# Queries and keys cast to bf16 in the DMA on GpSimd's queue and turned by single heads; values alone on SyncE's queue

## The chip, the cores and the metric

The kernel runs on one core of a Trainium2 chip. The metric is the device time of that core in microseconds (us), the median of several executions. Kernels are compared only within the same rounds. PE is TensorE, PEld its weight loads, DVE VectorE, ACT ScalarE, POOL GpSimd, SP SyncE.

## The reference, cut to what matters

Chunked attention with a few memory keys, then a Fourier mix of the whole batch entry, then an MLP:

```python
# q, k, v: (4, 8, 768, 64) fp32; mem_k, mem_v: (4, 8, 8, 64)
for c in range(24):                          # chunks of 32 queries
    k_full = concat(mem_k, k[l_start:r_end])   # 16 keys to the left, 8 to the right
    a = softmax(q_c @ k_full.T / 8)
    out[c] = a @ concat(mem_v, v[l_start:r_end])
x = out as (4, 768, 512)                     # heads side by side
u = x + real(fft2(x))                        # over sequence and model dimension
un = (u - mean) / sqrt(var + 1e-6)
out = u + relu(un @ w_ch1) @ w_ch2           # 512 -> 2048 -> 512
```

## The kernel before

Heads are worked in 16 pairs, four for each of the four batch entries ("batches"). Each task of an engine (a load, a cast, a turn, which is a transpose on TensorE, a product) is handed to a scheduler with a cost and its conditions; the scheduler fixes one static order for each engine. Within a batch the attention feeds the Fourier mix (DVE folds, TensorE products `ps`), and that the MLP (`ph` is the first product, `pc` the second). The MLP of batch 0 runs beside the attention of batch 1, and so on. Names in the traces: `trq` and `trk` are turned queries and keys, `va` values, `sc` scores, `e` exponentials, `xa` their products with the values, `xsb` the normalised sums; `zy`, `pq`, `ff`, `hi`, `lo` are steps of the folds. A PSUM bank, or bank, is one of the buffers that the kernel takes with `bank(...)` for TensorE's products (`trq`, `sc`, `xa`, `ps`, `ph` and others). The parts that matter here:

```python
def e_load_q(n):                     # e_load_k alike; both on SyncE's queue
    nc.sync.dma_start(qf[n % NS], q[...])              # fp32, 3 buffers
def e_load_v(n, hh):                 # also SyncE: 3 value pieces, the memory's values
    ...
def e_cast_q(n, eng):                # DVE in batch 0, GpSimd later; e_cast_k alike
    eng.tensor_copy(qb_of[n].rearrange(cp_b), qf[n % NS]...)   # fp32 -> bf16, one buffer
def e_overlap(n, hh):                # the rows that neighbouring chunks share
    nc.gpsimd.tensor_copy(v1[0:32, 1:NB, 0:D + 1], v1[96:128, 0:NT, 0:D + 1])
def e_turn_q(n):                     # 8 matmuls, both heads at once: 128 weight columns
    for j in range(RB):
        nc.tensor.transpose(trq[:, j*QP:(j+1)*QP], qb[:, j] as (p, h d), ident_b[...])
...
w2_sb = wpool.tile([P, NHT, DM], FP16)           # second MLP weight
va.append(w2_flat[...])                          # values of pair 3 lie in the same memory
W2_AT = (1, 1)                                   # w2 asked for with the second pair of batch 1
```

The softmax here doesn't subtract the row's maximum and nothing guards it: scores larger than these inputs give would overflow.

## Time and profile before

| | before |
|---|---|
| device time, median of 3 first runs | 317.24 us |
| span of the profiled run | 315.9 us |
| mean granted TensorE clock in it | 0.978 |
| PE / DVE / ACT / POOL busy | 295.4 / 188.1 / 168.8 / 80.7 us |
| first softmax exponential | 19.76 us |
| first MLP matmul | 56.41 us |
| waits of `pc` for `w2` | 3.6 us |

TensorE's busy share of 94% says little on its own. Early in the run it holds dummy matmuls that compute nothing (`warm`, 236 in the groups). I therefore read the time at milestones: the first exponential (the attention begins), the first MLP matmul (from there TensorE has real work nearly always), and each wait of TensorE behind it. A timeline line reads: start, length, engine, source line, operation, output<-input, shape, how many in a row, and in brackets the idle time before it with its releaser. The prediction below shows the lines of before.

### The profile page before, as it was taken

How to read it: one execution, taken by the hardware profiler on the slowest of the kernel's cores; microseconds unless marked ns; L12 is line 12 of the kernel's file. 1: busy time of each engine (PE TensorE's matmuls, PEld its weight loads, DVE VectorE, ACT ScalarE, POOL GpSimd, SP SyncE). 2: the span in 40 equal slices, each digit the busy share in tenths (PEclk: the TensorE clock that was granted, in tenths of full speed). 3: DMA queues.
4: the chain of work that ended last, by engine and by line, in shares of the span. 5: the costliest groups of instructions: out<-in, count | busy, mean ns of one | idle time of the engine just before them, and what ended most of it. 6: DMA issues, size and time to landing. Idle time of an engine off the chain costs nothing.

```text
span 315.9 us, 7464 instructions
## 1 busy us (share of the span) xinstructions
PE 295.4 (94%) x3129; PEld 197.9 (63%) x3129; DVE 188.1 (60%) x367; ACT 168.8 (53%) x302; POOL 80.7 (26%) x97
## 2 busy tenths in 40 slices
PE   8489899977999979999799999999999999999994
PEld 8488899644667656686466665666764554554541
DVE  8977989601454989789999598975940101002001
ACT  8778435873768844548547462851482270540710
POOL 6442811853333749333800001000020000000000
PEclk9779999999999979999899999999999999999999
DMA  7995999995397999253200000001000100101001
GB/s 191 193 174 116 245 211 211 191 246 102 81 196 145 193 187 208 63 161 95 58 0 2 35 0 36 35 0 66 2 33 29 74 0 37 65 0 68 33 33 66
DMA packets 41888, 30.68 MB, mean 97 GB/s; under 512 B 30080, under 2 KB 32128, under 8 KB 41856
## 3 DMA queue, kind: packets, MB, share of 16 engines
q1 hardware_dynamic: 35712, 19.73, 30.8%
q0 software_dynamic: 2688, 4.19, 7.5%
q10 hardware_dynamic: 3456, 6.29, 5.2%
q8 instruction: 24, 0.39, 0.6%
q14 instruction: 8, 0.07, 0.1%
HBM read 28.11 MB, written 6.29 MB: 109 GB/s over the span
## 4 chain that ended last, share of the span: by engine, by line
PE 73%; DVE 18%; DMA 5%; ACT 2%; issue 1%; DVEq 0%
PE pc L649 26%; PE ph L635 22%; PE ps L479 7%; PE xa L405 6%; PE pm L514 5%; DMA w_sb<-in_moe_w_ch_dram 5%; PE sc L380 2%; DVE xsb L416 2%; DVE zy L439 2%; DVE yS L689 1%; PE trk L359 1%; PE warm L428 1%; PE trq L346 1%; PE tp L614 1%; DVE pq L447 1%
## 5 line engine op out<-in xcount | busy, mean ns | idle before, releaser
L642 ACT ACTIVATE hT<-ph 128x384 f16<-128x384 f32 x128 | 62.0, 492 | 59.1 <-PE ph L635 58.4
L635 PE MATMUL ph<-unT,w_sb 128*128 128x384 f16 x512 | 90.7, 330 | 2.0 <-DVE unT L620 1.3
L649 PE MATMUL pc<-w_sb,hT 128*128 128x512 f16 x384 | 88.7, 379 | 3.6 <-DMA w_sb<-in_moe_w_ch_dram 3.6
L655 DVE SCALAR_TENSOR_TENSOR osb<-pc,rstd,xsb 128x512 f32<-128x512 f32 x24 | 18.0, 750 | 88.6 <-PE pc L649 88.5
L635 PEld LDWEIGHTS <-w_sb 128*128 128x128 f16 x512 | 49.1, 99 | 34.2 <-issue 4.5
L649 PEld LDWEIGHTS <-hT 128*128 128x128 f16 x384 | 36.0, 98 | 42.9 <-issue 4.1
L340 POOL COPY va<-va 32x780 f32<-32x780 f32 x30 | 32.6, 1097 | 39.1 <-DMA va<-in_v_dram 32.0
L392 ACT ACTIVATE e<-sc,mbias 128x384 f32<-128x384 f32 x62 | 32.7, 582 | 14.7 <-PE sc L380 14.5
L405 PEld LDWEIGHTS xa<-va,e 128*64 128x64 f32 x720 | 23.9, 140 | 8.0 <-issue 4.1
L405 PE MATMUL xa<-va,e 128*64 128x65 f32 x720 | 28.0, 229 | 0.0
L608 ACT ACTIVATE un<-xsb,mu_s 128x512 f16<-128x512 f32 x18 | 13.0, 721 | 16.4 <-DVE mu_s L602 16.3
L428 PE MATMUL warm<-zeros 128*128 128x128 bf16 x236 | 19.3, 247 | 1.0 <-DVE zero L246 1.0
L336 POOL CAST kb<-kf 104x1024 bf16<-104x1024 f32 x12 | 13.4, 1120 | 22.8 <-PE trk L359 10.8
L626 POOL TENSOR_SCALAR rstd<-mu_s 128x6 f32<-128x6 f32 x4 | 1.0, 245 | 71.4 <-DVE mu_s L602 71.3
L416 DVE TENSOR_TENSOR xsb<-xa,zs 128x384 f32<-128x384 f32 x32 | 17.8, 557 | 1.1
L428 PEld LDWEIGHTS <-zeros 128*128 128x128 bf16 x236 | 17.1, 113 | 1.4 <-DVE zero L246 1.0
L494 ACT CAST up<-ps 128x386 f16<-128x386 f32 x16 | 9.6, 601 | 14.9 <-PE ps L479 14.9
L332 POOL CAST qb<-qf 96x1024 bf16<-96x1024 f32 x12 | 13.3, 1106 | 15.2 <-PE xa L405 7.5
L601 DVE BATCH_NORM_STATS2 st<-xsb 128x6 f32<-128x512 f32 x24 | 16.5, 686 | 0.5
L467 ACT CAST hi<-ff 128x768 f16<-128x768 f32 x14 | 11.4, 833 | 9.7 <-DVE ff L560 6.7
L369 ACT COPY kTb<-trk 128x832 bf16<-128x832 bf16 x16 | 13.7, 856 | 5.1 <-PE trk L359 3.3
L351 ACT COPY qT<-trq 128x768 bf16<-128x768 bf16 x16 | 12.8, 802 | 6.1 <-PE sc L380 4.6
(134 smaller groups left out, 401.4 us busy)
## 6 DMA issues: line engine op xcount, KB each, us to landing
qf<-in_q_dram SPq DMA_DIRECT2D x16, 384.0 KB
kf<-in_k_dram SPq DMA_DIRECT2D x16, 384.0 KB
out_dram<-osb ACTq DMA_DIRECT2D x24, 256.0 KB
va<-in_v_dram SPq DMA_DIRECT2D x30, 176.0 KB
w_sb<-in_moe_w_ch_dram POOLq DMA_DIRECT2D x8, 512.0 KB, 12.1
va<-in_mem_v_dram SPq DMA_DIRECT2D x30, 24.0 KB
va<-in_v_dram SPq DMA_DIRECT2D x15, 28.0 KB
w_sb<-in_v_dram SPq DMA_DIRECT2D x2, 176.0 KB
```

Source lines behind the costliest of these rows:

```text
L340: nc.gpsimd.tensor_copy(v1[0:32, 1:NB, 0:D + 1], v1[96:128, 0:NT, 0:D + 1])
L392: nc.scalar.activation(e1[:, :, :, ts(half, 32)], sc[:, :, 0:6, ts(half, 32)], AFT.Exp, bias=mbias[:, half:half + 1], scale=1.0 / math.sqr ...
L405: nc.tensor.matmul(xa[64 * half:64 * half + 64, st, hh, 0:65], e1[:, hh, t6, :], v1[:, 6 * g + t6 + 1, 0:65], start=True, stop=True)
L416: nc.vector.tensor_tensor(xs[b][:, 3 * g:3 * g + 3, 2 * pr * D:(2 * pr + 2) * D] .rearrange("p s (h d) -> p s h d", h=2), xa[:, :, :, 0:D] ...
L428: nc.tensor.matmul(warm_of[0], zeros, zeros, start=True, stop=True)
L479: nc.tensor.matmul(out_[:, sp, :], part[:, ab, sp * 3 + st, c0:c1], tab[:, sp, st, :], start=(first and sp + st + i == 0), stop=(last and ...
L514: nc.tensor.matmul(pm[:, par, :], lhs, rhs[:, par, :], start=(im == 0), stop=(im == 3))
L601: nc.vector.bn_stats(st6, xs[b][:, kt, :])
L635: nc.tensor.matmul(ph[:, 0:384], w1_sb[:, dt, ts(ht, P)], unT_of[b][:, dt, sh * 384:(sh + 1) * 384], start=(dt == 0), stop=(dt == NDT - 1))
L642: nc.scalar.activation(hT_of[b, sh][:, ht, :], ph_of.pop((b, sh, ht))[:, 0:384], AFT.Relu, bias=0.0, scale=-1.0)
L649: nc.tensor.matmul(pc_of[b, sh, stl], hT_of[b, sh][:, ht, ts(stl, P)], w2_sb[:, ht, :], start=(ht == 0), stop=(ht == NHT - 1))
L655: nc.vector.scalar_tensor_tensor(osb, pc_of.pop((b, sh, stl)), rstd_of[b][:, st:st + 1], xs[b][:, st, :], ALU.mult, ALU.add)
```

## The change

Its intent: let the DMA cast queries and keys, so that neither DVE (batch 0) nor GpSimd (later) casts; keep four pairs in flight instead of three; leave SyncE's queue to the values; take the values' last tile out of the fixed memory of `w2`, and load `w2` earlier. The price is that the DMA leaves the two heads side by side in another order, so each head is turned by itself: 16 matmuls with 64 weight columns for each turn instead of 8 with 128.

```diff
-    NS = 3
+    NS = 4
-    qf = [spool.tile([QP, 2, RB * D], FP32, ...)]     # kf alike
+    qf = [spool.tile([QP, 2, RB * D], BF16, ...)]     # kf: slices of one tile
 def e_load_q(n):                                      # e_load_k alike
-        nc.sync.dma_start(qf[n % NS], ...)
+        nc.gpsimd.dma_start(qf[n % NS], ...)
-    def e_cast_q(n, eng): ...
-    def e_cast_k(n, eng): ...
 def e_turn_q(n):                                      # e_turn_k alike
-            nc.tensor.transpose(trq[:, j*QP:(j+1)*QP], qb[:, j] as (p, h d), ...)
+            for hh in range(2):
+                nc.tensor.transpose(trq[64*hh:64*hh+64, j*QP:(j+1)*QP],
+                                    qb[:, hh, ts(j, D)], ident_b[0:QP, 0:QP])
 ...
-    t_rows = ...                      # GpSimd's clears of value tiles came before the tables
+    # clears moved to ACT, SyncE (a DMA) and behind GpSimd's table rows
+        behind1 = kept["ov"] if n == HP else None
+    done = {0: fourier(0)}
+    t_w2 = load_w2(kept["f0"])
-            if (b, i) == W2_AT:
-                t_w2 = load_w2(kept["ov"])
```

More of the change, by code (lines that the diff above doesn't have):

```diff
@@ L173 @@
     bps = ctx.enter_context(tc.tile_pool(name="banks", bufs=1, space=bass.MemoryType.PSUM))
-    NS = 3
+    NS = 4
     HP = H // 2
-    qf = [spool.tile([QP, 2, RB * D], FP32, name=f"qf{i}") for i in range(NS)]
-    kf = [spool.tile([KP, 2, RB * D], FP32, name=f"kf{i}") for i in range(NS)]
+    qf = [spool.tile([QP, 2, RB * D], BF16, name=f"qf{i}") for i in range(NS)]
+    kf_all = spool.tile([KP, NS, 2, RB * D], BF16)
+    kf = [kf_all[:, i] for i in range(NS)]
     NV = 3
@@ L186 @@
            for pr in ((0, 3, 1, 2) if b == 0 else (0, 2, 1, 3))]
-    plan = Plan(dict(qf=NS, kf=NS, va=NV, kTb=NKT, qb=1, kb=1, qT=2, tr=2, sc=1, xa=2, e1=3,
+    plan = Plan(dict(qf=NS, kf=NS, va=NV, kTb=NKT, qT=2, tr=2, sc=1, xa=2, e1=3,
                      xsb=3, fold=2, hl=1, up=4, dn=4, acc=4, mlp=3, un=3, unT=2, hT=1, osb=3), 6)
@@ L196 @@
     MLPS = 1000000
+    QT_DVE = (1, 2)
     NPR = B * H // 2
@@ L212 @@
     sv0 = cpool.tile([P, 1], FP32)
+    gate = cpool.tile([1, 1], FP32)
     zero = cpool.tile([P, 1], FP32)
@@ L232 @@
     w1_sb = wpool.tile([P, NDT, DFF], FP16)
-    w2_sb = wpool.tile([P, NHT, DM], FP16)
-    w2_flat = w2_sb.rearrange("p a b -> p (a b)")
-    va.append(w2_flat[:, 0:4 * NB * 66].bitcast(FP32)
-              .rearrange("p (h b c) -> p h b c", h=2, c=66))
-    e1_last = (w2_flat[:, 4 * NB * 66:4 * NB * 66 + 4 * 6 * 64].bitcast(FP32)
-               .rearrange("p (h t c) -> p h t c", h=2, c=64))
+    last = wpool.tile([P, 2, NB * 66 + 6 * 64], FP32, tag="w2", name="last")
+    va.append(last[:, :, 0:NB * 66].rearrange("p h (b c) -> p h b c", c=66))
+    e1_last = last[:, :, NB * 66:].rearrange("p h (t c) -> p h t c", c=64)
+    w2_of = []
     def va_at(n):
@@ L272, in e_scales, with e_clear_kf @@
         nc.vector.tensor_scalar(svD, sv[:, 0:1], 1.0 / DM, None, ALU.mult)
+    def e_clear_kf():
+        for p0, p1 in ((0, 7), (7 + QP, KP)):
+            nc.sync.dma_start(kf_all[p0:p1].rearrange("p i h (j d) -> p (i h j) d", d=P),
+                              zeros[0:p1 - p0].unsqueeze(1).to_broadcast(
+                                  [p1 - p0, NS * 2 * RB * D // P, P]))
     def e_clear_act(t):
-        flat = t if len(t.shape) == 2 else t.rearrange("p a b -> p (a b)")
-        nc.scalar.copy(flat, zero[0:flat.shape[0]].to_broadcast(list(flat.shape)))
+        nc.scalar.copy(t, zero[0:t.shape[0]].unsqueeze(2).to_broadcast(list(t.shape)))
     def e_rows_of_ones():
@@ L300, in e_load_q @@
         b, pr = seq[n]
-        nc.sync.dma_start(qf[n % NS],
+        nc.gpsimd.dma_start(qf[n % NS],
                           q[b, 2 * pr:2 * pr + 2].rearrange("h (p j) d -> p h (j d)", j=RB))
@@ L305, in e_load_k @@
         b, pr = seq[n]
-        nc.sync.dma_start(kf[n % NS][7:7 + QP],
+        nc.gpsimd.dma_start(kf[n % NS][7:7 + QP],
                           k[b, 2 * pr:2 * pr + 2].rearrange("h (p j) d -> p h (j d)", j=RB))
@@ L323, in e_load_v @@
                           mem_v[b, 2 * pr + hh].unsqueeze(1).to_broadcast([NMEM, NT, D]))
-    qT_of, kT_of, qb_of, kb_of, tr_of, e1_of, sc_of, xa_of, xs = ({} for _ in range(9))
-    cp_q = "p h (j d) -> p h j d"
-    cp_b = "p j h d -> p h j d"
-    def e_cast_q(n, eng):
-        qb_of[n] = apool.tile([QP, RB, 2, D], BF16, tag="qb", bufs=1, name="qb")
-        eng.tensor_copy(qb_of[n].rearrange(cp_b), qf[n % NS].rearrange(cp_q, j=RB))
-    def e_cast_k(n, eng):
-        kb_of[n] = apool.tile([KP, RB, 2, D], BF16, tag="kb", bufs=1, name="kb")
-        eng.tensor_copy(kb_of[n].rearrange(cp_b), kf[n % NS].rearrange(cp_q, j=RB))
+    qT_of, kT_of, tr_of, e1_of, sc_of, xa_of, xs = ({} for _ in range(7))
     def e_overlap(n, hh):
@@ L342, in e_turn_q @@
     def e_turn_q(n):
-        qb = qb_of.pop(n)
+        qb = qf[n % NS]
         tr_of[n] = trq = bank([P, S], BF16, "trq")
         for j in range(RB):
-            nc.tensor.transpose(trq[:, j * QP:(j + 1) * QP],
-                                qb[:, j].rearrange("p h d -> p (h d)"), ident_b[0:QP, 0:QP])
+            for hh in range(2):
+                nc.tensor.transpose(trq[64 * hh:64 * hh + 64, j * QP:(j + 1) * QP],
+                                    qb[:, hh, ts(j, D)], ident_b[0:QP, 0:QP])
     def e_qT(n):
         qT_of[n] = qT = apool.tile([P, S], BF16, tag="qT", bufs=2, name="qT")
-        nc.scalar.copy(qT.rearrange("p (a j) -> p a j", j=RB),
-                       tr_of.pop(n).rearrange("p (j a) -> p a j", j=RB))
+        (nc.vector.tensor_copy if n in QT_DVE else nc.scalar.copy)(
+            qT.rearrange("p (a j) -> p a j", j=RB),
+            tr_of.pop(n).rearrange("p (j a) -> p a j", j=RB))
     def e_turn_k(n):
-        kb = kb_of.pop(n)
+        kb = kf[n % NS]
         trk = bank([P, RB * KP], BF16, "trk")
@@ L358, in e_turn_k @@
         for j in range(RB):
-            nc.tensor.transpose(trk[:, j * KP:(j + 1) * KP],
-                                kb[:, j].rearrange("p h d -> p (h d)"), ident_b[0:KP, 0:KP])
+            for hh in range(2):
+                nc.tensor.transpose(trk[64 * hh:64 * hh + 64, j * KP:(j + 1) * KP],
+                                    kb[:, hh, ts(j, D)], ident_b[0:KP, 0:KP])
     def e_mkT(n):
@@ L648, in e_ch2 @@
         for ht in range(4 * part, 4 * part + 4):
-            nc.tensor.matmul(pc_of[b, sh, stl], hT_of[b, sh][:, ht, ts(stl, P)], w2_sb[:, ht, :],
+            nc.tensor.matmul(pc_of[b, sh, stl], hT_of[b, sh][:, ht, ts(stl, P)], w2_of[0][:, ht, :],
                              start=(ht == 0), stop=(ht == NHT - 1))
@@ L663 @@
     t_warm = add("PE", 6.0, lambda: e_warm(56), [t_zero], rank=-1, take=("mlp",))
-    t_iota = add("POOL", 0.7, e_iota)
+    t_iota = add("POOL", 0.7, e_iota, rank=-2)
     t_first = add("ACT", 1.4, e_first_sine, [t_zero])
     t_clear = {}
-    t_clear["kf", 0] = add("DVE", 0.9, lambda: nc.vector.memset(kf[0], 0.0))
-    t_id = add("POOL", 0.5, lambda: make_identity(nc, ident))
-    for hh in range(2):
-        t_clear["va", 0, hh] = add("ACT", 0.85, lambda hh=hh: e_clear_act(va[0][:, hh]), [t_zero])
-    t_clear["kf", 1] = add("ACT", 1.0, lambda: e_clear_act(kf[1]), [t_zero])
+    t_clear["kf"] = add("SP", 1.4, e_clear_kf, [t_zero], moved=0.3, rank=-4)
+    t_id = add("POOL", 0.5, lambda: make_identity(nc, ident), rank=-1)
+    for i, hh in ((0, 0), (0, 1), (1, 0), (1, 1), (2, 0)):
+        t_clear["va", i, hh] = add("ACT", 0.85, lambda i=i, hh=hh: e_clear_act(va[i][:, hh]),
+                                   [t_zero])
     t_scales = add("DVE", 0.2, e_scales, [t_iota])
@@ L699, with e_gate @@
                                                   None, ALU.bitwise_and), t3)
-    for hh in range(2):
-        t_clear["va", 1, hh] = add("ACT", 0.85, lambda hh=hh: e_clear_act(va[1][:, hh]), [t_zero])
-    t_clear["kf", 2] = add("ACT", 1.0, lambda: e_clear_act(kf[2]), [t_zero])
-    t_masks = add("POOL", 0.9, e_masks, [t_angle["S"]])
-    for i in range(2, NV + 1):
-        for hh in range(2):
-            t_clear["va", i, hh] = add("POOL", 0.9, lambda i=i, hh=hh: nc.gpsimd.memset(
-                va[i][:, hh], 0.0), [t_angle["D"]])
-    for i in range(1, NV + 1):
-        t_ones[i] = add("DVE", 0.1, lambda i=i: e_ones(i),
-                        [t_col, t_clear["va", i, 0], t_clear["va", i, 1]])
+    def e_gate():
+        nc.gpsimd.tensor_copy(gate, yD[0:1, 0, 0:1])
+    t_gate = add("POOL", 0.1, e_gate, [t_angle["D"]])
+    t_masks = add("POOL", 0.9, e_masks, [t_gate])
+    t_clear["va", 2, 1] = add("DVE", 0.8, lambda: nc.vector.memset(va[2][:, 1], 0.0), rank=130)
     def e_sines(part):
@@ L740 @@
     t_rows = add("POOL", 1.9, e_table_rows, [t_sines[2]], rank=125)
+    for hh in range(2):
+        t_clear["va", 3, hh] = add("POOL", 0.9, lambda hh=hh: nc.gpsimd.memset(va[3][:, hh], 0.0),
+                                   [t_rows], rank=126)
+    for i in range(1, NV + 1):
+        t_ones[i] = add("DVE", 0.1, lambda i=i: e_ones(i),
+                        [t_col, t_clear["va", i, 0], t_clear["va", i, 1]])
     t_neg = [add("DVE", 0.4, lambda i=i: e_neg(i), t_sines[:2], rank=140 + i,
@@ L753, in attention @@
         b, pr = seq[n]
-        lq = add("SP", 0.45, lambda: e_load_q(n), take=("qf",), moved=1.5, rank=10 * n)
-        lk = add("SP", 0.4, lambda: e_load_k(n), [t_clear["kf", n] if n < NS else None],
+        behind1 = kept["ov"] if n == HP else None
+        lq = add("POOL", 0.8, lambda: e_load_q(n), [behind1, kept.get("lk")], take=("qf",), moved=1.5, rank=10 * n)
+        lk = add("POOL", 0.8, lambda: e_load_k(n), [t_clear["kf"], lq],
                  take=("kf",), moved=1.5, rank=10 * n + 1)
+        kept["lk"] = lk
         lv = [add("SP", 2.1 if hh == 0 else 1.4, lambda hh=hh: e_load_v(n, hh),
-                  [t_ones.get(n)], rank=10 * n + (5 if n == HP - 1 else 15) + hh,
+                  [t_clear.get(("va", n, 0)), t_clear.get(("va", n, 1))], rank=10 * n + 2 + hh,
                   take=("va",) if hh == 0 and n != HP - 1 else (), moved=1.6) for hh in range(2)]
@@ L763, in attention @@
         mgp, mg, mgl = SPARE[b]
-        ce, cn, cc = (nc.vector, "DVE", 0.68) if first else (nc.gpsimd, "POOL", 1.04)
-        cq = add(cn, cc, lambda: e_cast_q(n, ce), [lq, calm], take=("qb",), give=("qf",), margin=mgl)
-        ck = add(cn, cc, lambda: e_cast_k(n, ce), [lk, calm], take=("kb",), give=("kf",), margin=mgl)
         ov = [add("POOL", 0.84, lambda hh=hh: e_overlap(n, hh), [lv[hh], calm], margin=mgl) for hh in range(2)]
@@ L769, in attention @@
         behind = kept.get("v0") if b == 1 else None
-        tq = add("PE", 0.40, lambda: e_turn_q(n), [cq, t_idb, behind], take=("tr",), give=("qb",),
+        tq = add("PE", 0.40, lambda: e_turn_q(n), [lq, t_idb, behind, kept.get("tk")], take=("tr",), give=("qf",),
                  margin=mgp)
-        eq = add("ACT", 0.80, lambda: e_qT(n), [tq], take=("qT",), give=(("tr", tq),),
+        eq = add("DVE" if n in QT_DVE else "ACT", 0.80, lambda: e_qT(n), [tq], take=("qT",), give=(("tr", tq),),
                  margin=mg)
-        tk = add("PE", 0.43, lambda: e_turn_k(n), [ck, t_idb, behind], take=("tr",), give=("kb",),
+        tk = add("PE", 0.43, lambda: e_turn_k(n), [lk, t_idb, behind, tq], take=("tr",), give=("kf",),
                  margin=mgp)
+        kept["tk"] = tk
         mk = add("DVE", 0.2, lambda: e_mkT(n),
@@ L798, in attention @@
         return x_
-    t_mkf = add("SP", 0.7, e_mkf, moved=0.8, rank=12)
+    t_mkf = add("SP", 0.7, e_mkf, moved=0.8, rank=-5)
     t_mkb = add("DVE", 0.22, lambda: nc.vector.tensor_copy(
@@ L814 @@
     ov_last = kept["ov"]
-    W2_AT = (1, 1)
     w2v = moe_w_ch2.rearrange("(ht p) m -> p ht m", p=P)
@@ L823, in load_w1, with e_w2 @@
             for dt in range(NDT)]
+    def e_w2(g):
+        if g == 0:
+            w2_of.append(wpool.tile([P, NHT, DM], FP16, tag="w2", name="w2_sb"))
+        nc.gpsimd.dma_start(w2_of[0][:, ts(g, 4), :], w2v[:, ts(g, 4), :])
     def load_w2(after):
-        return [add("POOL", 0.7, lambda g=g: nc.gpsimd.dma_start(
-            w2_sb[:, ts(g, 4), :], w2v[:, ts(g, 4), :]), [after], moved=3.5, rank=-1)
-            for g in range(4)]
+        return [add("POOL", 0.7, lambda g=g: e_w2(g), [after], moved=3.5, rank=-1)
+                for g in range(4)]
     def part_of_later(b, add, t_rest):
```

## The prediction

> **What bounds the kernel now.** I read the page first: the engines in slices and the chain that ended last.
>
> ```profile
> PE   8489899977999979999799999999999999999994
> ...
> DVE  8977989601454989789999598975940101002001
> ...
> PEclk9779999999999979999899999999999999999999
> ...
> PE 73%; DVE 18%; DMA 5%; ACT 2%; issue 1%; DVEq 0%
> ```
>
> TensorE looks full from the start, but early on that is filler: the groups list 236 "warm" matmuls, which compute nothing. The chain says what counts: TensorE for 73%, DVE for 18%, and 5% on the load of the second weight matrix. So I split the span into stretches.
>
> ```profile
> 0.00:36.00 36.00, 28.85 (x537) 26.75 (x538) 31.38 (x69) 27.68 (x42) 18.19 (x38) 0.91 0.84 181
> 36.00:56.40 20.40, 20.15 (x254) 18.64 (x254) 18.67 (x49) 8.64 (x15) 5.34 (x5) 1.00 1.12 214
> 56.40:76.00 19.60, 16.01 (x124) 9.46 (x124) 4.22 (x13) 13.79 (x27) 12.20 (x14) 1.00 1.05 190
> 76.00:100.00 24.00, 24.00 (x390) 15.26 (x390) 10.64 (x22) 16.23 (x30) 8.52 (x9) 1.00 0.55 128
> ```
>
> Columns: stretch, length, busy us of PE, PE weight load, DVE, ACT, POOL, then PE clock, DMA share, GB/s. Up to 56.4 us (first MLP matmul) DVE is busy 31.38 + 18.67 = 50.05 of 56.4 us: a front that DVE, ACT and the loads set. From 56.4 to 76 TensorE is busy 16.0 of 19.6: 3.6 us of real idling. Afterwards it is full, except near 112 to 116 and 152 to 156 (1.65 and 2.26 busy of 4 each, clock dropping to 0.73 and 0.61 in the next 4 us). So three places matter: the front, the 3.6 us, and every microsecond of TensorE work after about 56 us, which adds nearly one for one.
>
> The timeline of the front (start, length) and two lists of waits:
>
> ```profile
> 2.87 3.10 DVE L676 CAST ident_b<-ident 128x128 bf16<-128x128 f32 x1
> 3.00 3.82 DVE L689 TENSOR_SCALAR yS<-tri,svS 128x386 f32<-128x386 f32 x3
> 12.24 0.68 DVE L332 CAST qb<-qf 96x1024 bf16<-96x1024 f32 x1
> 12.98 1.33 DVE L336 CAST kb<-kf 104x1024 bf16<-104x1024 f32 x1
> 19.76 1.05 ACT L392 ACTIVATE e<-sc,mbias 128x384 f32<-128x384 f32 x2
> 35.28 1.06 ACT L392 ACTIVATE w_sb<-sc,mbias 128x384 f32<-128x384 f32 x2
> ```
> ```profile
> PE pc L649 <- DMA w_sb<-in_moe_w_ch_dram: 3.6, 3, 1.9
> ...
> SPq L321 <- DMA w_sb<-in_v_dram: 3.8, 1, 3.8
> ```
>
> The first softmax exponential runs at 19.76 because the casts queue on DVE behind the sine tables (done at 12.25), and turning, copying and a table load follow. The eighth runs at 35.28. The second wait is SyncE's: values aliased onto the weight tile stop that queue, and the DMA share in 22 to 28 us is 0.53, 0.00, 0.70.
>
> [...] the weights, the only loads with a cast, are the only bytes on q0. [...] beside GpSimd's casts and copies at 100 to 115 us zy takes 2.08 and 1.58 us against 1.02 alone, pq 1.67 against 0.95. [...]
>
> **The change part by part.**
>
> Casts go. DVE loses, before 30 us, four q casts (2.7 us) and four k casts (3.4) and a clear of kf (0.91), and gains two qT copies (about 0.8 each if as on ACT) and one clear of a va half (under 0.9): net about -4.5. GpSimd's early va and weight-tile clears, beside which the ident_b cast took 3.10 us and three yS steps 3.82 (0.48 each for the like step on tri), move behind the tables: perhaps 2 us more. I put the tables' end at 9.6 to 10.6 instead of 12.25. q and k can be turned before that, so ACT goes from its seven sines (4.9 us) straight into the 1.28 us table load and the first exponential, at about 14 instead of 19.76. From there one exponential, one score matmul and one wait repeat every 1.9 to 2.0 us (26.55, 28.48, 30.47): seven of those plus a copy put the eighth at 28.5 to 29, against 35.28. ACT's own work in it, 8 x 1.05 + 3 x 0.85 + 0.8 = 11.8 us, fits.
>
> Values alone on SyncE, and the weight tile no longer aliased. A pair's six value DMAs take SyncE about 3.6 us to issue (6.47 to 10.5 for the first), so the fourth, whose clear now waits for the table rows, is issued by about 20. Transfer: the trace's 256 B packets average 26.4 ns, 1744 per pair or 2.9 us over 16 engines; uncast q and k average 130 ns, 384 packets or 3.1 us. Cast weights with 2048 B written average 103 ns, so 1024 B written should take perhaps 52 to 65: 1.3 to 1.6 us per pair (estimate). Four pairs are then about 17.5 us instead of 24. The last values should land near 23, not 31, and not hold the exponentials.
>
> So the front shortens by 5.5 to 7.5 us; I take 6.5.
>
> w2 is asked for when the first Fourier stage ends (about 46 us on the old clock), not at 57.8. Its packets cost 13.2 us of 16 engines, so even behind q and k it should land before its first use (67.6 old). The 3.6 us go: -3.6.
>
> GpSimd loses 24 casts of 1.04 us or more in batches 1 to 3, 25 us of reading SBUF beside DVE. In the DVE-led stretch at 100 to 116 the excess over the undisturbed lengths is 0.7 + 0.6 + 1.1 + 0.6 + 0.6 = 3.6 us; half the GpSimd work there is casts, half overlap copies that stay. With a little at 150: -2.3.
>
> TensorE pays: each of q and k is turned by 16 matmuls with 64 weight columns instead of 8 with 128.
>
> ```profile
> L405 PE MATMUL xa<-va,e 128*64 128x65 f32 x720 | 28.0, 229 | 0.0
> ...
> L359 PE MATMUL trk<-ident_b,kb 104*128 104x104 bf16 x128 | 9.3, 220 | 0.0
> L346 PE MATMUL trq<-ident_b,qb 96*128 96x96 bf16 x128 | 8.8, 216 | 0.9 <-DVE qb L332 0.9
> ```
>
> The means are latencies; starts are what counts. In the trace single trq matmuls start 42.5 ns apart and trk 46: their 96 and 104 columns, weight load hidden. The xa matmuls with 64 weight columns run as pairs in the two column halves, 7 ns apart, but a pair comes only every 58.3 ns, although 65 columns stream in 27. Load and stream are then serial, 58.3 - 27 = 31 ns for the load. The new turns have that shape (two heads, two halves): 31 + 40 = 71 ns per pair for q, 31 + 43 = 74 for k, against 42.5 and 46. That is 8 x 28.5 = 0.23 us more per turn. Turns of the first four pairs lie in filler; the other 12 pairs have 24: 5.5 us. A change of array shape costs about 0.1 us (eight trq take 0.45 after xa, 0.34 otherwise). Going through the neighbours of each later turn I count 17 more changes: 1.7. Sum 7.2; about a sixth falls into stretches that wait for DVE: +6.0.
>
> Sum: -6.5 - 3.6 - 2.3 + 6.0 = -6.4 on the span of 315.9, so 309.5. The median run of before is 1.3 above that span: 310.8. As q and k are also prefetched one pair deeper, I state 310.5.
>
> **The rivals.** (a) The turns eat everything: if heads do not overlap in the column halves, 16 matmuls take twice the old 0.34 to 0.37 at best and 16 x 71 ns = 1.14 at worst, +0.35 to +0.8 per turn, 8 to 19 us over 24: time 313 to 322. For it: load and stream are serial in xa. Against: xa's pairs do overlap, and the change alternates halves in the same way. (b) The software queue becomes the bound: w1, the next q and k, and w2 now share one queue[...]. Before, four w1 issues took 2.42 us and w2 3.00, its last piece landing about 15 us later. If batch 1's keys wait behind 4 MB of w1, TensorE idles 2 to 4 us near 50: 312 to 315. Against: the DMA share falls, and w1 moves forward with the front. (c) The front gains less, because DVE's remaining work is the limit: tables to 9.6, then about 20 us up to the last norm, so near 31 in any case against 38.5; that alone caps the gain near 7. [...] (d) More is gained: without casts and their single buffers TensorE's two gaps (about 7 us with the slow clock) close: 305.
>
> **Range and chances.** Front, +-2; turns, +-3; gaps behind 100 us, +-3, because the static order changes[...]: together about +-5. Range 304.5 to 316.5. Two per cent faster is below 310.9, almost on my estimate: 0.51 faster, 0.46 same, 0.03 slower.
>
> **What would show it.** First exponential near 14 and eighth near 29; first ph near 50 instead of 56.4; no wait of pc for w_sb; 256 trq and 256 trk matmuls with 64 columns, pairs 71 to 75 ns apart, a turn in 0.57 to 0.70 us; GpSimd without casts and zy, pq, lo nearer 1.0 us; q0 near 10.5 MB and q1 without 2 KB packets. I am wrong if a pair takes much over 80 ns, if TensorE waits for q or k after 45 us, if the tables end after 12, or if the gaps near 112 and 152 grow.

## The result, and the profile after

The kernel after took 307.61 us (307.16 to 308.47, 4 runs), beside 318.01 us (314.67 to 319.69, 4 runs) for before: ratio 0.971, 95% interval 0.963 to 0.979. A ratio here is the mean time of one kernel's fast runs over that of the other's of the same rounds, so it is not quite the ratio of the medians quoted. Five more rounds, later, gave 307.60 beside 317.32 us, ratio 0.969 (0.966 to 0.972). The prediction, 310.5 with 304.5 to 316.5, holds the result, and "faster" was its likelier side. The sum inside it is another matter.

The page of the kernel after: engines in slices, the granted clock, the DMA queues (packets, MB, share), the chain that ended last.

```profile
PE   7759999999999999998889999999999999999994
...
DVE  8728989603521998799996979856911001001001
...
PEclk9999999999999999999999999999999999999998
...
q0 software_dynamic: 9344, 10.49, 21.4%
q1 hardware_dynamic: 29335, 7.21, 12.6%
...
PE 81%; DVE 6%; ACT 5%; DMA 3%; POOL 1%; issue 1%; SPq 1%; ACTq 0%; POOLq 0%
```

DVE's share of the chain fell from 18% to 6%, and the dips in the row of the clock (two 7s, a 7 and an 8 beside 9s before) are gone. The prediction's sum has no term for the second fact.

The stretches of the kernel after, columns as in the prediction:

```profile
0.00:36.00 36.00, 28.59 (x643) 25.74 (x644) 25.98 (x68) 25.31 (x39) 21.59 (x49) 1.00 0.77 134
...
54.20:76.00 21.80, 21.73 (x348) 14.14 (x349) 6.88 (x21) 19.84 (x38) 8.32 (x12) 1.00 1.00 157
100.00:120.00 20.00, 20.00 (x271) 12.62 (x267) 19.07 (x31) 12.63 (x23) 6.14 (x6) 1.00 0.32 79
```

DVE is freed in the front (31.38 to 25.98 us), and TensorE has no hole any more from 54 to 76 us and around 112 us. Yet the front itself hardly shortened. Its timeline in the kernel after:

```profile
8.59 3.47 SPq L329 DMA_DIRECT2D va<-in_mem_v_dram  x1
...
14.99 1.05 ACT L392 ACTIVATE e<-sc,mbias 128x384 f32<-128x384 f32 x2
...
16.40 0.83 POOL L337 COPY va<-va 32x780 f32<-32x780 f32 x1 [4.74 <-DMA va<-in_v_dram]
...
21.30 1.06 ACT L392 ACTIVATE e<-sc,mbias 128x384 f32<-128x384 f32 x2
...
33.38 1.05 ACT L392 ACTIVATE last<-sc,mbias 128x384 f32<-128x384 f32 x2
```

The first exponential came at 14.99, 4.8 us earlier, as predicted. But GpSimd then waited 4.74 us for the first values, the third exponential came only at 21.30, the eighth at 33.38 (35.28 before), and the first MLP matmul at 54.16 (56.41 before). One issue on SyncE's queue alone took 3.47 us while GpSimd's queue was pouring in all four pairs' queries and keys; later issues of the same line took 0.72 us (20.15 and 23.97), and with two pairs held back (an experiment below) the same issue took 0.70 us.

The groups of the turns in the kernel after (count, busy us, mean ns; then the idle time before them):

```profile
L359 PE MATMUL trk<-ident_b,kf_all 104*64 104x104 bf16 x256 | 8.9, 211 | 1.4 <-DVE qT L349 1.3
L344 PE MATMUL trq<-ident_b,qf 96*64 96x96 bf16 x256 | 8.4, 208 | 1.0 <-DMA qf<-in_q_dram 0.7 <-ACT qT L349 0.3
```

Twice as many matmuls, and no more busy time than the 9.3 and 8.8 us of before.

To see where 9.9 us of span went, I added up the intervals between the starts of TensorE's matmuls from the first MLP matmul to the end, and split what exceeds the streaming time (columns over 2.4 per ns and 3 ns more, as the starts at full clock say: 216 ns apart for `pc`'s 512 columns, 56 for the 128 of `warm`, 42.5 for the 96 of `trq`; for `xa` these sums leave its half-rate part among the small gaps):

| us | before | after | difference |
|---|---|---|---|
| up to the first MLP matmul | 56.41 | 54.16 | -2.25 |
| waits (over 0.25 us) | 10.54 | 4.40 | -6.14 |
| of these: at `pc` for `w2` | 4.06 | 0 | -4.06 |
| of these: first `ps` of batch 1 | 2.51 | 0 | -2.51 |
| lost in stretches at half clock, small gaps there included | 3.71 | 0 | -3.71 |
| turns: matmuls and the gaps beside them | 9.81 | 12.38 | +2.57 |
| other small gaps | 14.99 | 14.78 | -0.21 |

The four kinds behind the first MLP matmul make -7.5 (waits, half clock, turns, other gaps; the spans of this part differ by 254.98 - 247.43 = 7.55), and with the front -9.8. Half clock itself can have cost no more than half of the two stretches of 3.41 us, 3.4 us.

### The profile page after: what moved, and what is told of

Its sections match the earlier page's. It is cut to its first block, busy times and chain, and to the rows that moved or that the text cites.

```text
span 306.0 us, 7950 instructions
## 1 busy us (share of the span) xinstructions
PE 291.3 (95%) x3391; PEld 193.9 (63%) x3391; DVE 172.9 (56%) x361; ACT 166.7 (54%) x299; POOL 65.2 (21%) x104
## 3 DMA queue, kind: packets, MB, share of 16 engines
q1 hardware_dynamic: 29335, 7.21, 12.6%
## 4 chain that ended last, share of the span: by engine, by line
PE 81%; DVE 6%; ACT 5%; DMA 3%; POOL 1%; issue 1%; SPq 1%; ACTq 0%; POOLq 0%
PE pc L649 27%; PE ph L635 26%; PE ps L479 9%; PE xa L405 7%; PE pm L514 4%; DMA va<-in_v_dram 3%; PE sc L380 2%; PE trk L359 2%; PE warm L428 1%; DVE st L601 1%; PE trq L344 1%; DVE xsb L595 1%; PE tp L614 1%; ACT e L392 1%; ACT hi L467 1%
## 5 line engine op out<-in xcount | busy, mean ns | idle before, releaser
L635 PE MATMUL ph<-unT,w_sb 128*128 128x384 f16 x512 | 88.8, 326 | 1.8 <-ACT hT L642 1.2
L392 ACT ACTIVATE e<-sc,mbias 128x384 f32<-128x384 f32 x62 | 32.7, 582 | 13.5 <-PE sc L380 13.1
L337 POOL COPY va<-va 32x780 f32<-32x780 f32 x30 | 26.7, 905 | 46.0 <-DMA va<-in_v_dram 45.9
L405 PE MATMUL xa<-va,e 128*64 128x65 f32 x720 | 26.6, 225 | 2.5 <-POOL va L337 1.4
L405 PEld LDWEIGHTS xa<-va,e 128*64 128x64 f32 x720 | 23.1, 138 | 7.4 <-issue 3.7
L608 ACT ACTIVATE un<-xsb,mu_s 128x512 f16<-128x512 f32 x18 | 13.0, 723 | 14.0 <-DVE mu_s L602 13.9
L428 PE MATMUL warm<-zeros 128*128 128x128 bf16 x242 | 17.3, 229 | 1.0 <-DVE zero L247 1.0
L428 PEld LDWEIGHTS <-zeros 128*128 128x128 bf16 x242 | 14.9, 103 | 1.9 <-DVE zero L247 1.0
L415 DVE RECIPROCAL zs<-xa 128x6 f32<-128x6 f32 x32 | 6.1, 189 | 16.2 <-PE xa L405 16.2
L472 DVE TENSOR_TENSOR lo<-ff,hi 128x768 f16<-128x768 f32 x14 | 14.5, 1039 | 1.3 <-ACT hi L467 1.3
L349 ACT COPY qT<-trq 128x768 bf16<-128x768 bf16 x14 | 11.2, 797 | 7.0 <-PE sc L380 4.9
```

The source lines that it names most:

```text
L392: nc.scalar.activation(e1[:, :, :, ts(half, 32)], sc[:, :, 0:6, ts(half, 32)], AFT.Exp, bias=mbias[:, half:half + 1], scale=1.0 / math.sqr ...
L405: nc.tensor.matmul(xa[64 * half:64 * half + 64, st, hh, 0:65], e1[:, hh, t6, :], v1[:, 6 * g + t6 + 1, 0:65], start=True, stop=True)
L428: nc.tensor.matmul(warm_of[0], zeros, zeros, start=True, stop=True)
L635: nc.tensor.matmul(ph[:, 0:384], w1_sb[:, dt, ts(ht, P)], unT_of[b][:, dt, sh * 384:(sh + 1) * 384], start=(dt == 0), stop=(dt == NDT - 1))
```

## The experiments

Twelve kernels ran; all gave correct results. My theory after reading the traces: the turns are nearly free; all four pairs' queries and keys crowd the first values out of the front; casts on GpSimd cost DVE and with it TensorE; and a part of the gain is the granted clock. The rival for each: the prediction's own step, or that the effect lies off the path.

### Turns alone (before, turned by single heads)

```diff
-            nc.tensor.transpose(trq[:, j*QP:(j+1)*QP], qb[:, j] as (p, h d), ...)
+            for hh in range(2):
+                nc.tensor.transpose(trq[64*hh:64*hh+64, j*QP:(j+1)*QP], qb[:, j, hh], ...)
```

> The kernel before with one part of the change alone: queries and keys still come uncast on SyncE's queue and GpSimd still casts them, but they are turned by single heads, 16 matmuls of 64 weight columns a turn instead of 8 of 128. Prediction's step (a head costs a weight load that nothing hides, 0.23 us a turn more, and more mode changes): about 6 us slower, 324 us beside 318. Rival, from the trace after (two heads' matmuls 42 to 46 ns apart together): the loads are hidden, 24 turns add under 1 us, 317 to 319.5 us, the same. If it is 6 us slower, the change got more elsewhere than the traces let me find.

Measured: 317.59 beside 317.77 us, ratio 1.0006 (0.9935 to 1.0078). Six us more would be 1.019, so the prediction's step is refuted. Behind the first MLP matmul, turns and the gaps beside them rose from 9.81 to 10.93 us, thus 1.1 us: 0.2 in the matmuls, 0.9 in gaps at changes of array shape. This profile happened to have no half-clock stretch in the middle, so its total hides that cost. Its front was 2.3 us longer (58.74 us), which isn't laid to the turns: DVE's first query cast began at 13.40 and took 1.89 us (12.24 and 0.68 before), and it did so too in a later experiment (first try on the clock) that doesn't touch the turns.

### A probe of the array's rates (after, with blocks of dummy matmuls at the start)

```diff
-    t_warm = add("PE", 6.0, lambda: e_warm(56), ...)
+    # 16 ordinary ones, then blocks of 20 with 64 weight columns:
+    # fp32 / bf16, 65 / 96 / 128 columns, halves by turns; then 96 columns in one half
```

> The kernel after with the start's dummy matmuls replaced by blocks of 20 small ones with 64 weight columns: fp32 and bf16, 65, 96 and 128 columns, in the two column halves by turns, then in one half. The prediction took the 58.3 ns of an xa pair (fp32) for 31 ns of load plus 27 ns of stream and gave the bf16 turns the same load. (i) If fp32's load is serial, a pair takes 58 ns at 65 columns, 71 at 96, 85 at 128. (ii) If fp32 streams at half rate and its load is hidden, 58, 84 and 111. bf16: if its load of 64 columns is serial, 71 ns at 96 columns; if hidden, 42.5. In one half alone: hidden loads would keep 42.5 per single bf16 matmul of 96 columns.

Read from the starts in the trace, at full clock:

| | 65 columns | 96 | 128 | 96, one half only |
|---|---|---|---|---|
| fp32, per pair of records (one half: per record) | 58.3 ns | 82.5 | 109 | 82.5 |
| bf16, per pair of records (one half: per record) | 31 ns | 42.4 | 56 | 42.4 |

```profile
2.80 5.77 PE L671 MATMUL warm<-zerof 128*64 128x65 f32 x120
8.40 1.47 PE L671 MATMUL warm<-zeros 128*64 128x65 bf16 x60
9.70 3.47 PE L671 MATMUL warm<-zerof 128*64 128x96 f32 x40
```

Mind what a record is: the first row holds three fp32 blocks of 20 calls each and has 120 records, the second three bf16 blocks with 60. An fp32 matmul thus leaves two records, each of twice the bf16 time: 20 calls of 96 columns took 1.65 us in fp32 and 0.42 in bf16, four times as long. The `xa` products are such fp32 calls (12 calls, 24 records a group).

Reading (ii) holds for a record: fp32 takes twice the columns' time, and the load of 64 columns is hidden in both types. The 58.3 ns of a pair of `xa` records, on which the prediction built 31 ns of load, are two times 65 columns at 2.4 per ns (54 ns) and a few ns. Two heads in the two halves take what one matmul takes, so 16 matmuls cost what 8 did. (309.93 us; the longer start isn't of interest.)

### Early `w2` alone (before)

```diff
+    t_w2 = load_w2(kept["f0"])         # behind the first Fourier stage's folds
-            if (b, i) == W2_AT: t_w2 = load_w2(kept["ov"])
```

> The kernel before with one thing alone: the 2 MB of w2 are asked for behind the first Fourier step instead of ten heads in; everything else, casts and queues too, as before. Prediction's step: the wait of the second MLP product for w2 (3.6 us in the chain) goes, so 314 to 315 us beside 318, ratio about 0.988. Rival: the wait only stood in place of another (TensorE would have waited for the last h there, or the earlier load slows the pairs' loads), under 1 us gained, ratio over 0.997.

Measured: 315.62 beside 317.77 us, ratio 0.9953 (0.9859 to 1.0047). No `pc` waits for `w2` in its trace, but a new wait stands later on TensorE:

```profile
117.59 0.35 PE L380 MATMUL sc<-qT,kTb 64*128 64x64 bf16 x12 [1.41 <-ACT e L392]
```

and from 144 to 148 us TensorE was busy for 0.97 us of 4, with a half-clock stretch behind it (mean clock 0.66 from 148 to 152 us):

```profile
147.03 0.65 PE L359 MATMUL trk<-ident_b,kb 104*128 104x104 bf16 x8 [3.35 <-POOL kb L336]
```

The span behind the first MLP matmul fell by 2.1 us (254.98 to 252.84), not by 3.6. But the waits over 0.25 us there add up to 10.50 us beside 10.54: inside the old kernel the whole wait moved on, 3.35 us of it to a cast on GpSimd. What the profile gained is mostly half clock, one stretch of 3.41 us instead of two. The time alone can't tell the gain from none.

### `w2` late again (after, one part undone)

> The kernel after with one part undone: the 2 MB of w2 are asked for ten heads in, as in the kernel before. Theory (the earlier w2 is worth its 3.6 us of waits): the second MLP product waits 3 to 4 us for w2 again, 310.5 to 311.5 us beside 307.6[...]. Rival: TensorE has other work then, or w2 on the emptier queue still lands in time, under 1 us slower.

```diff
-    t_w2 = load_w2(kept["f0"])
+            if (b, i) == (1, 1): t_w2 = load_w2(kept["ov"])
```

Measured: 308.70 us (307.67 to 310.62), ratio to before 0.9737 (0.967 to 0.981). The wait did not come back: from the first MLP matmul on, the span is 247.44 us against 247.43. The rival holds by the trace; the time, some 1 us above the kernel after's by the ratios, lies at the rival's limit. (The profiled run's front was slower by 1.8 us, with a half-clock stretch of 6.8 us in it; the two runs at a clock of 0.994 took 307.67 and 308.25.) Why it works late is to be seen in GpSimd's timeline. Before:

```profile
55.48 0.84 POOL L340 COPY va<-va 32x780 f32<-32x780 f32 x1 [4.07 <-DMA va<-in_v_dram]
57.06 0.83 POOL L340 COPY va<-va 32x780 f32<-32x780 f32 x1 [0.74 <-DMA va<-in_v_dram]
57.84 0.78 POOL L826 DMA_DIRECT2D w_sb<-in_moe_w_ch_dram  x1
```

In this experiment:

```profile
51.62 3.00 POOL L827 DMA_DIRECT2D w_sb<-in_moe_w_ch_dram  x4
```

The issue of `w2` stands in GpSimd's order behind its copies of values. Before, those waited for values that came late on SyncE's shared queue. With values alone there, the same place in the order is reached 6.2 us earlier: 17.3 us before the first `pc` (68.91) instead of 9.8 (67.59), and what moved it, by the waits, is the queues: from 38 us up to the issue GpSimd waited 15.7 us for values before, 3.9 us here (and 7.0 us with the issues of its own queries and keys). Early issue and separate queues each remove the wait.

### Casts on GpSimd again (after, with dummy casts)

```diff
+        if n >= HP:
+            for t, rows in ((tq, QP), (tk, KP)):
+                add("POOL", 1.04, cast of a spare fp32 tile to a spare bf16 tile, [t, calm])
```

> The kernel after, and GpSimd makes two dummy casts of fp32 to bf16 for each of the 12 later pairs, of the size of those that the change took away; nothing waits for them. Theory A (DVE's relief): DVE slows beside them (pq back from 0.95 to 1.1 us, zy from 1.10 to 1.16), the wait of TensorE for the second batch's fold near 112 us comes back with 1 to 2.5 us[...]: 309.5 to 311.5 us beside 307.6. Theory B (the order of the work and the earlier loads closed that gap): DVE slows a little, the time stays within 0.7 us and the mean granted clock stays over 0.99.

Measured: 310.78 us (310.43 to 311.81), ratio to before 0.9801 (0.974 to 0.986), about 3 us above the kernel after by its ratio of 0.969 to 0.971. The part behind the first MLP matmul is 2.0 us longer (249.41), with one wait of 1.03 us on DVE near 105 us. The same group of DVE's folds from 54 to 240 us, in the kernel after and here:

```profile
L447 DVE TENSOR_TENSOR pq<-zy 128x768 f32<-128x768 f32 x6 | 5.7, 950 | 0.0
```
```profile
L450 DVE TENSOR_TENSOR pq<-zy 128x768 f32<-128x768 f32 x6 | 7.2, 1196 | 0.0
```

Theory A holds in the main: casts that nothing waits for cost 2.0 us behind the first MLP matmul, with slower `pq` steps in front of the wait. Two of its details missed: the wait near 112 us did not come back, so what closed that one stays open, and `zy` did not slow down (1105 and 1027 ns), so not every step of DVE is slower in the mean. Of the 3 us of time up to 1 lies elsewhere: this kernel also clears the dummy casts' input on DVE at the start, and its first exponential came at 15.62 instead of 14.99. One half-clock window stood in its front too, but the kernel after had one there in most of its runs; I don't count it.

### The granted clock, first try (before, dummy matmuls in two waits)

```diff
-    t_warm = add("PE", 6.0, lambda: e_warm(56), ...)
+    t_warm = add("PE", 6.0, lambda: e_warm(120), ...)
 def e_rows(b, par, ab):
+        if (b, par, ab) == (1, 0, 0):
+            for i in range(36): nc.tensor.matmul(ps[:, 0, 0:P], zeros, zeros, ...)
```

> The kernel before, with dummy matmuls in two of TensorE's waits and nothing else: 64 more behind the starting ones (they fill 9 to 12.4 us) and 36 ahead of the second batch's first Fourier product (2.0 of the 2.4 us of wait near 112). Theory (part of the change's gain is the granted clock[...]): the stretches at half clock at 12.4 to 19.2 and 114.8 to 118.2 us go, the mean granted clock rises from 0.978 to 0.99 or more, and the time falls by 2 to 4 us, to 314 to 316, with no load, cast or turn changed. Rival (the slow stretches lie in waits anyway): the clock rises and the time stays within 0.7 us of 317.8.

Measured: 318.24 beside 316.26 us, ratio 1.003 (0.994 to 1.012). It failed as an experiment:

```profile
117.21 2.18 PE L487 MATMUL ps<-zeros 128*128 128x128 bf16 x36 [1.97 <-DVE xsb L416]
```

The dummies waited themselves, for the PSUM bank that DVE's normalisation frees, and then stood in the way. In the front they ended at 11.7 us and the wait went on to 15.5, and the clock still fell (0.94 in the mean of the first 56 us, 0.94 to 56.4 us in the kernel before). It tells nothing of the clock's worth, but it tells what the wait near 112 us is for: a bank, freed by a DVE held up.

### The granted clock, second try (before, dummies in a bank already held)

```diff
 def e_ch1(b, sh, ht):
+        if (b, sh, ht) == (0, 1, 15):        # its bank's columns 384 to 511 are never read
+            for i in range(36): nc.tensor.matmul(ph[:, 384:512], zeros, zeros, ...)
```

> The kernel before with 36 dummy matmuls (2.0 us) behind the last matmul of the first batch's first MLP product, in columns of its PSUM tile that nobody reads, so that they run in the wait of about 2.4 us that follows; the earlier attempt's dummies waited for the same PSUM bank as the work and filled nothing. Theory (the wait[...] costs a half-clock window besides): the first Fourier products of batch 1 start 80 to 85 ns apart instead of 160, no half-clock stretch between 100 and 140 us, 1 to 1.5 us less, about 316.3 beside 317.7. Rival: the wait's end is what counts and the clock comes back in other waits, within 0.5 us; or the dummies lengthen the wait and it is 0.5 to 2 us slower.

Measured: 316.00 (314.99 to 316.27, 6 runs) beside 317.32 us, ratio 0.9953 (0.9926 to 0.998): 1.3 us faster by doing useless work. The kernel before at this place, TensorE's timeline:

```profile
114.78 0.34 PE L479 MATMUL ps<-cosS,hi 128*128 128x193 f16 x1 [2.35 <-DVE xsb L416]
...
115.08 0.37 PE L479 MATMUL ps<-cosS,hi 128*128 128x193 f16 x1
115.24 0.37 PE L479 MATMUL ps<-cosS,lo 128*128 128x193 f16 x1
...
119.10 0.24 PE L479 MATMUL ps<-sinS,lo 128*128 128x193 f16 x1
119.18 0.25 PE L479 MATMUL ps<-sinS,hi 128*128 128x193 f16 x1
```

After the wait, like matmuls start 160 ns apart; once the clock is back, 80 to 90. With the dummies:

```profile
112.39 2.17 PE L640 MATMUL ph<-zeros 128*128 128x128 bf16 x36
114.40 1.03 PE L652 MATMUL pc<-w_sb,hT 128*128 128x512 f16 x4
115.39 0.26 PE L479 MATMUL ps<-cosS,hi 128*128 128x193 f16 x1
...
115.57 0.25 PE L479 MATMUL ps<-cosS,hi 128*128 128x193 f16 x1
115.66 0.25 PE L479 MATMUL ps<-cosS,lo 128*128 128x193 f16 x1
```

The products start 85 ns apart at once, and no half-clock stretch lies between 100 and 140 us. The wait itself was not shortened: the products start 47.5 us behind the first `pc`, 47.2 before. So such a wait (2.35 us here, with TensorE busy for 1.07 of the 3.41 us before the half clock) is paid twice in the kernel before, once as the wait and once as half clock behind it (114.8 to 118.2 us). Which waits are followed by half clock changes from execution to execution: this profile had no stretch near 155 us, but one from 70.8 to 74.3, behind a wait of 2.36 us for `w2`. The 1.3 us are thus a mean over executions.

The records agree. In the kernel before, half clock was granted from 12.4 to 19.2, 114.8 to 118.2 and 155.7 to 159.2 us: 6.83 + 3.41 + 3.41 us, in all 13.65, and (1 - 0.978) x 2 x 315.9 = 13.9. All its executions together: the two at a mean clock of 0.968 took 319.3 and 319.9 us (the second is slow), those at 0.987 to 0.989 took 314.2 to 316.3; that is its spread. The six repeated runs of the kernel after had 0.993 to 0.999.

### Three kernels on the front (after)

First, queries and keys of pairs 2 and 3 held back:

```diff
-        behind1 = kept["ov"] if n == HP else None
+        behind1 = kept["ov"] if n == HP else kept["ovs"][n - 2] if 2 <= n < HP else None
```

> The kernel after, but queries and keys of pairs 2 and 3 are asked for only once the value tiles of pairs 0 and 1 are complete; the queues, casts and turns stay. Theory (the front gained 2.3 us and not 6.5 because all four pairs' queries and keys on GpSimd's queue kept the 16 DMA engines busy from 4 to 16 us and the first values, alone on SyncE's queue, landed only at 16.2): the first values land by about 12, the third exp comes at 17 to 18 instead of 21.3, the last lo of batch 0 ends near 40.5 instead of 43.5, and the time falls by about 3 us, to 304.5. Rival (what limits the values is SyncE's own pace, one pair in 3.7 to 4.5 us, or what GpSimd must do for them): the first values come earlier but the eighth exp stays at 32 to 33.5, under 1 us gained.

Measured: 309.18 (307.61 to 310.65) beside 317.77 us, ratio 0.9752 (0.968 to 0.983): no gain over the kernel after, which its interval includes. The first values' copy began at 13.5 instead of 16.4 and the third exponential came at 19.06, but the eighth only at 33.29. What was held back now came too late: the turns waited 1.31 us (21.18) and 0.73 us (25.93) for queries, because eight clears of GpSimd's table rows stood between pair 0's two copies, and the release of pair 2 with them. The theory was half right, and the rival's figure for the eighth exponential is the one measured.

Second, the same with GpSimd's table rows and the last pair's clears behind the copies:

```diff
+        if n == 0:  the clears of the last value tile come after pair 0's copies
+        if n == 1:  the table rows come after pair 1's copies
```

> As the kernel with pairs 2 and 3 held back, and besides GpSimd's table rows and the last pair's clears come after its copies of overlaps for pairs 0 and 1, so that no memset stands between those copies. Theory: TensorE's two waits of 1.1 and 1.4 us for the first value tiles shrink; another 0.5 to 1.5 us off, about 303.5 us. Rival: the exps of the third to eighth head are paced by the values' landing alone, and this one equals the other within 0.5 us.

Measured: 306.43 (305.86 to 307.58) beside 317.77 us, ratio 0.967 (0.960 to 0.974): not the 303.5 expected, but 2.8 us under the first version, so GpSimd's order counts beside it. To settle so small a difference it was run again beside the kernel after, and with the order of GpSimd changed alone:

> The kernel after unchanged, run beside the next two so that they are compared on one chip. Expected: 307 to 308.5 us, every run with a mean granted clock of 0.994 or more (no half-clock stretch but the one after the end), while the runs of the kernel before spread over 314 to 320 us with clocks of 0.968 to 0.989, the longer the lower the clock.

> The kernel with pairs 2 and 3 held back and GpSimd's table rows moved behind, once more. Its eighth exp came 3.5 us and its first matmul of the MLP 3.8 us before those of the kernel after, its span was only 1.9 us shorter. Theory: TensorE had filled the wait for values with turns that must now be done later, so what counts is the idle time of TensorE over the whole span (14.7 us after, 12.5 here): 1 to 2.2 us below the kernel after in the same rounds. Rival: the difference was chance, within 0.7 us.

> The kernel after with only GpSimd's order changed (table rows behind pair 1's copies, the last pair's clears behind pair 0's); all four pairs' queries and keys are asked for at once, as in the kernel after. If the first values' landing at 16.2 us sets the front, the third exp moves from 21.3 only to 19 or 20 and the time stays within 0.7 us of the kernel after. If the memsets between the two copies set it, the gain of e3b appears here too: 306.4 us.

Measured, five rounds on one chip:

| | median us (runs) | ratio to before | mean clock of the runs |
|---|---|---|---|
| kernel after | 307.60 (6) | 0.9689 (0.966 to 0.972) | 0.993 to 0.999 |
| GpSimd's order alone | 307.49 (6) | 0.9687 (0.965 to 0.972) | 0.989 to 1.0 |
| both | 306.36 (5) | 0.9656 (0.963 to 0.968) | 0.997 to 1.0 |

The expectation that the kernel after has no half-clock stretch missed: its repeated profile had one from 19.3 to 22.7 us, in the front, and a clock of 0.994 in most runs says the same. Timeline of the version with both, repeated run:

```profile
12.63 1.71 POOL L337 COPY va<-va 32x780 f32<-32x780 f32 x2 [2.15 <-ACT kTb L369]
14.29 0.65 POOL L308 DMA_DIRECT2D qf<-in_q_dram  x1
...
16.31 0.90 POOL L337 COPY va<-va 32x780 f32<-32x780 f32 x1
```

The first two value copies run together at 12.6, and pair 2's queries are asked for at 14.3. The third exponential comes at 17.94 (22.13 in the repeated run of the kernel after) and the first MLP matmul at 50.95 instead of 53.92. Neither half suffices: with GpSimd's order alone the first values still landed late (first copy 15.54, third exponential 21.03). The pair of changes makes a version that beats both kernels by the medians, 306.4 us against 307.6 and 317.3.

Of the 3 us at the first MLP matmul, 1.2 arrive at the end. My theory for that, in the expectation, was that turns had only been put off. It falls: TensorE's matmul time behind that point is the same in both (192 and 176 turn matmuls each). What grew there are waits, 4.43 to 5.39 us, and small gaps at turns and elsewhere, 0.9 us more. That is how the rest was lost; which resource of the later stage is behind it I did not test.

## Why the prediction was right or wrong

Its verdict and range were right, its value 2.9 us high. It came out by errors that cancel, which is luck; point by point in the order of its sum.

**Front, -6.5: wrong, -2.25.** The failed step is "the last values should land near 23, not 31, and not hold the exponentials". The first half of the step held: tables done at 9.99 (9.6 to 10.6 predicted), first exponential 14.99 (14). Then the first values landed at 16.2 and the last at about 28.8, and they did hold the exponentials. Two things went into this. One is arithmetic: the estimate of 52 to 65 ns for a cast packet took the packets of the weights, 103 ns, for 2048 bytes written; they have 1024, as the queries' cast packets do, and those took 106 ns. A pair's 384 packets are therefore 384 x 106 / 16 = 2.5 us, not 1.3 to 1.6. The other is order: SyncE's queue was freed of queries and keys, but the 16 DMA engines were not (their share read 1.11 to 1.26 from 4 to 16 us), and GpSimd's queue put all four pairs' ahead of the first values. Shown by the two-part experiment: holding pairs 2 and 3 back and clearing GpSimd's way gave 3.0 to 3.8 us at the first MLP matmul. Rival (c) was right that the front gains less, with another cause.

**`w2`, -3.6: right in size, the cause incomplete.** The waits are gone (-4.06 by starts). But the earlier issue isn't needed for it in the new kernel, as the late version showed, and in the old kernel it alone removed no waiting in sum (10.50 us beside 10.54).

**GpSimd's casts gone, -2.3: right in size.** Dummy casts cost 2.0 us behind the first MLP matmul. The wait of 2.5 us near 112 is closed in the kernel after; that the casts alone had made it isn't shown, since the dummies brought 1.03 us near 105 instead.

**Turns, +6.0: wrong, +1.1 alone and +2.6 in the changed kernel.** The failed step is "Load and stream are then serial, 58.3 - 27 = 31 ns for the load". It read an fp32 rate as a bf16 load. The load term of 5.5 us (4.6 in the sum) measured 0.2 to 0.6; the changes of array shape, 1.7 x 5/6 = 1.4 in the sum, measured 0.9 to 2.0, so that term was sound. The predicted sign (pairs 71 to 75 ns apart) read 42 to 46 ns.

**The granted clock, no term: -3.7.** The prediction quotes the dips near 116 and 156 us and prices only the waits in front of them. Rival (d) names "the slow clock" in passing and says 305. The dummies in one wait showed it: 1.3 us for one window, as a mean over executions.

Together: predicted -6.4; the front gave 4.25 less, the turns cost 3.4 less, the clock added 3.7, and the rest 0.6; -6.4 + 4.25 - 3.4 - 3.7 - 0.6 = -9.9, the difference of the profiled spans. Rivals (a) and (b) did not occur: TensorE waited 0.7 us for queries in all.

## What to carry to other kernels

Before pricing an operation by another one's interval, check that type and rate are the same: a half-rate fp32 stream looks just like a hidden cost (58.3 ns for a pair of records at 65 fp32 columns, 31 in bf16). A wait of TensorE like the one of 2.35 us here should be priced with the half clock that can follow it (3.41 us here), and was worth filling even with dummies (1.3 us gained), which sat in a bank already held; those that waited for a bank gained nothing (ratio 1.003). Moving loads to another queue did not by itself make room for what stayed: the first values landed at 16.2 us while the DMA share read 1.11 to 1.26, and holding two pairs of queries and keys back let their copy begin at 13.5 instead of 16.4. So the order in which all queues are fed should put first what is needed first.

## What these traces show of the hardware

- The granted clock: in the kernel before, the full-clock stretches between half-clock ones last 95.57, 37.55 and 157.01 us, 28, 11 and 46 times 3.413 us, and the half-clock ones within its span 3.41 or 6.83. Of the windows of that length at full clock in these 14 traces, all 13 with up to 1.50 us of busy time were followed by half clock, and of those with 1.63 us and more only one was (1.89 us). In the kernel before, the windows in front of half clock held 0.00, 1.07 and 1.89 us of busy time, the emptiest others 1.63 and 2.40. Behind the first MLP matmul, the four single waits of 2.35 to 3.36 us were each followed by half clock, the three of 1.83 to 1.97 us were not.
- Loads of 64 weight columns behind 96 bf16 columns cost nothing that the probe shows: 42.4 ns for each matmul in one array half or for a pair in both, beside 42.5 ns for one matmul with 128 weight columns in the kernel before.
- A call in fp32 leaves two records in the trace, each of twice the bf16 time (82.5 against 42.4 ns at 96 columns): 1.65 us for 20 calls of 96 columns against 0.42 in bf16.
- The price of a cast in the DMA: a packet with 1024 B written and cast took 106 ns, an uncast one of 2048 B 130 ns, so the cast halves the bytes written and saves a fifth of the time.
- A busy q0 and a stretched issue on SyncE's queue came together: one issue of SyncE took 3.47 us while the DMA share was 1.2 (2.74 in the repeated run), and 0.70 and 0.72 us in the two versions that hold two pairs back.
